# Between attention and the first expert layer: four weight loads issued later, two gathers moved into one branch, three buffers cleared at another place

## The chip, the cores and the metric

The kernel runs on one core of a Trainium2 chip. The metric is the time of one execution on the device in microseconds (us), the median of several runs. Five engines work side by side, each with its own queue of instructions that it takes in order: TensorE (PE, matrix products and transposes), VectorE (DVE), ScalarE (ACT), GpSimd (POOL) and SyncE (SP). SP and POOL also start transfers between main memory and on-chip memory: SP the plain ones, POOL the indirect ones, which read or write rows at addresses that stand in a table. Instructions wait for each other by counters.

## The reference

Attention over 2 x 8 heads of 576 positions with a mask in blocks of 64, then two layers of mixture of experts with 8 experts each, on 1152 tokens of 512 values (inner width 1024; `capacity` is 288):

```python
    scores = scale * np.matmul(q, k.transpose(0, 1, 3, 2))
    mask = block_i >= block_j
    scores = np.where(mask, scores, -1000000000.0)
    scores = scores - np.max(scores, axis=-1, keepdims=True)
    attn = np.exp(scores)
    attn = attn / (np.sum(attn, axis=-1, keepdims=True) + 1e-09)
    return np.matmul(attn, v).astype(np.float32)
...
    logits = x @ w_gate
    expert_idx = np.argmax(logits, axis=1)
...
        if counts[e] < capacity:
            disp[e, counts[e]] = x[i]
...
    h = np.maximum(np.einsum('ecd,edf->ecf', disp, w1), 0.0)
    y = np.einsum('ecf,efd->ecd', h, w2)
...
            out[i] = gate_w[i] * y[expert_idx[i], pos[i]]
```

Here `gate_w` is the softmax value of the chosen expert. The second layer works on the result in the same way, but sends each token to the two experts with the highest noisy logits and adds their weighted outputs.

## The kernel before

The kernel works in three stages one behind the other: attention, the eight experts of the first layer, the eight of the second. The stretch of this study is the seam between the first two.

**Weights.** Each expert has eight units of 512 KB, four of `w1` and four of `w2`. A unit is loaded by SP into one of seven buffers `raw0` to `raw6` (`load`, lines 148 to 159), and then split into a high part (ACT, line 167) and a low part (DVE, in two halves, line 170), which PE reads. As soon as DVE is through with a buffer, `split` issues the load that comes next into the same buffer (`behind(u)`). The last unit of each expert is not split; it goes to a buffer `wf` of its own. Units are numbered through the experts; `turn[u]` is the place of a unit in the order of splits. `HELD` (6) and `AHEAD` (5) are the first eleven places: those units are split during attention. Five of their buffers are loaded again behind the last rows of attention, with the units at the places 13 to 17; those at 14 to 17 are the four `w1` units of expert 2, which are split beside the work of expert 1.

**Attention's end.** The rows of attention are stored to main memory (`x_d`, lines 405 and 406). A table `T1` says which rows belong to which expert. The first 128 rows of expert 0 are also picked out directly on PE (L822), so that expert 0 can begin before anything has been fetched. The other rows are fetched by POOL with `row1(e, blk, n)` (line 1441), in blocks of 128, 128 and 32 rows, into `xr[e, blk]`, which has two sets of buffers (even and odd experts). Rows beyond an expert's count are left out by a bounds check.

**The experts of layer 1.** For each expert there are two branches, one for up to 128 tokens (`one_block`; its lines 1043 to 1080) and one for more (`large`, with `blocks`). Before the branch stands what both share. Inside a branch a planner (`Flow`) puts the operations of expert e, the splits of the weights for the next expert (`splits`), the transposes of the next expert's fetched rows (`prep`, lines 1015 to 1021), and the after-work of the expert before (`post`) into one order for each engine, by estimated costs. Its estimate of when a load has landed is a table (`came`), which the change does not touch. The result of expert e is scaled into `px` on ACT (line 1206), which reads the gate from the fetched rows `xr[e, 0]`.

**Three buffers `gs`** take the rows that layer 2 fetches. They are cleared once by POOL (line 1546).

Of the kernel before, what the change touches and what calls it, by code (L numbers as in the profile page):

```python
# [46 lines left out]
def attention_moe_moe2(ctx, tc, q, k, v, wg1, w1a, w2a, cap, wg2, wn2, noise, w1b, w2b, out):  # L47
    nc = tc.nc
    B, H, S, D = q.shape
    E, DM, F = w1a.shape  # L50
# [4 lines left out]
    XW = DM + 12  # L55
# [4 lines left out]
    SLOTS, RAWS, MORE = 13, 5, 2  # L60
# [5 lines left out]
    EARLY, HELD = 8 - WHOLE, 6  # L66
# [69 lines left out]
    def behind(u):  # L136

        i = turn[u] + (RAWS if turn[u] < HELD else RAWS + MORE)
        return order[i] if i < len(order) else None
# [8 lines left out]
    def load(u, q=nc.sync):  # L148
        if u is None or u >= NU:
            return  # L150
        m, r = divmod(u, 8 * E)
        e, i = divmod(r, 8)
        w1, w2 = (w1a, w2a) if m == 0 else (w1b, w2b)
        t = wfull[u % 8 - EARLY] if whole(u) else raw(u)
        if i < 4:
            q.dma_start(out=t, in_=w1[e, i * 128:(i + 1) * 128, :])
        else:
            f = (i - 4) * 256
            q.dma_start(out=t.rearrange("p (a d) -> p a d", a=2),
                              in_=w2[e, f:f + 256, :].rearrange("(a p) d -> p a d", p=128))  # L160

    def split(u, part=None, follow=True):
        if u >= NU:
            return
        t, h, l = raw(u), whi[slot(u)], wlo[slot(u)]
        if part in (None, 0):
            nc.scalar.activation(h, t, AF.Copy)  # L167
        if part != 0:
            c = {1: slice(0, 512), 2: slice(512, 1024), 3: slice(0, 1024), None: slice(0, 1024)}[part]
            (nc.gpsimd if part == 3 else nc.vector).tensor_sub(l[:, c], t[:, c], h[:, c].bitcast(F32))  # L170

            if part != 1 and follow:
                load(behind(u))

    def w1_at(e, kk, f0, f1):
        s = slot(8 * e + kk)
# [120 lines left out]
    with ExitStack() as actx:  # L297
# [564 lines left out]
        def split_op(i, deps=(), after=()):  # L862
            u = order[i]
            a = AT.add("split", "A", 0.95, lambda op: split(u, 0), list(deps) + [made["raw", i]])
            v1 = AT.add("split", "V", 0.6, lambda op: split(u, 1), [a], behind=after)
            made["split", i] = AT.add("split", "V", 0.6, lambda op: split(u, 2, False), [v1, a])
            made["raw", i + RAWS] = AT.add("load", "S", 0.1, lambda op: load(behind(u)), [made["split", i]], dma=1.5, drawn=False, behind=[made["stored"]] if i >= HELD else ())

        ctx.enter_context(tc.manual_schedule())
        made["load", 0] = AT.add("load", "S", 0.0, lambda op: None, dma=6.0, lag=-3.6)  # L870
# [568 lines left out]
    def row1(e, blk, n):  # L1439
        t = xr[e, blk] = xrs[e % 2][blk]  # L1440
        others("read", "sent", nc.gpsimd.indirect_dma_start(
            out=t[:n], out_offset=None, in_=x_d, in_offset=_off(T1[:n, 3 * e + blk:3 * e + blk + 1]),
            bounds_check=NT - 1, oob_is_err=False))

    for u in range(EARLY, 8):
        load(u)
    for e, i in ((1, 0), (0, 1), (0, 2), (1, 1), (1, 2), (0, 0)):
        row1(e, *BLK[i])
    nc.vector.memset(T2[:, 0], float(NT))
    nc.vector.memset(T2[:, 1], 0.0)  # L1450
    for _, _, t in pend[0:2]:
# [18 lines left out]
    for e in range(E):  # L1470
        for u in range(8 * e + EARLY, 8 * e + 8) if e else ():
            load(u)
        if e + 1 == E:
            F = Flow()
            total(F, cnt0, None)
            F.run()

        def beside(F, first):
            done = splits(F, units(e))
            nxt = post(F, first, last=True)[0] if first is not None else None  # L1480
            if e + 1 < E:
                for blk, n in BLK:
                    d = F.add("G", 1.04, lambda blk=blk, n=n: row1(e + 1, blk, n)) if e else None
                    prep(F, lambda blk=blk: xr[e + 1, blk], n, xT[(e + 1) % 2], 128 * blk, deps=[d], when=(WHEN0 if e == 0 else F.par["when"]) + 1.5 * blk)
            else:
                d, _ = rows2(F, (0, 0), 0, 0, tis[0])
                prep(F, lambda: G[0, 0][2], 128, xT[0], 0, deps=[d])
            return done, nxt

        last = None if e == 0 else pend[(e - 1) % 2]  # L1490
        cur = pend[e % 2]
        mt = [xr[e, i][:, DM:XW] for i in range(3)]
        n_e = many1(e)
        if e == 0:
            for r in regs[0].handles:
                nc.reg_load(r, cnt1[0:1, 0:1])

        def busy(bank, n):

            for _ in range(n):  # L1500
                nc.tensor.matmul(bank, hT[0][:, 0, 0:128], whi[slot(8 * e + 4)][:, 0:512], start=True, stop=True)

        def begin(F):

            def go():
                for r in regs[(e + 1) % 2].handles:
                    nc.reg_load(r, cnt1[0:1, e + 1:e + 2])
                tc.mark_branch_hint_location(f"first{e + 1}", hint=many1(e + 1) > 128, engines=[mybir.EngineType.PE])

            if e + 1 < E:  # L1510
                F.add("P", 0.4, go, tail=30.0, after=2.5)

        def large():
            F = Flow(LARGE)
            begin(F)
            done, nxt = beside(F, last)

            def fin(y, blk, p, first):
                r = to_pend(F, y, 128, lambda: mt[blk], 3 * e + blk, (pend[2], cur)[blk], p, first)
                if blk == 0:  # L1520
                    post(F, pend[2], deps=r, ranks=nxt)

            here = [prep(F, lambda blk=blk: xr[0, blk], n, xT[0], 128 * blk) for blk, n in BLK[1:]] if e == 0 else ()
            blocks(F, e, xT[e % 2], R, fin, done=done, deps=here)
            F.close(F.run())
            with tc.If(n_e > 256):
                F = Flow()
                _, z, _, tl = post(F, cur)
                product2(F, e, 2, lambda y, blk, p, first: to_pend(F, y, R, lambda: mt[2], 3 * e + 2, cur, p, first, deps=[z, tl["sent"]]))
                w = F.add("P", 1.6, lambda b: busy(b, 7), ends, take="h")  # L1530
                F.add("P", 0.0, lambda: None, [w], frees=w)
                F.run()

        with tc.If(n_e > 128, label=f"first{e}") as cmp:
            large()
        with cmp.Else():
            F = Flow(SMALL if e else FIRST)
            begin(F)
            done, nxt = beside(F, last)
            one_block(F, e, xT[e % 2], 128, lambda y, n, p, first: to_pend(F, y, n, lambda: mt[0], 3 * e, cur, p, first), done=done)  # L1540
            F.close(F.run())
        came, later = later, ({}, {})
        state["u"] = min(NU, 8 * e + 8 + EARLY)
        if e == 0:
            for i in range(3):
                nc.gpsimd.memset(gs[i], 0.0)


    mctx.close()
# [262 lines left out]
```

## Time and profile before

| | us |
|---|---|
| median of 3 runs (lowest, highest) | 547.79 (546.66, 547.98) |
| the profiled execution's own time | 548.82 |
| its span, first to last instruction | 547.2 |
| PE busy | 514.5 (94%) |
| DVE busy | 379.1 (69%) |
| ACT busy | 294.1 (54%) |
| POOL busy | 143.1 (26%) |

The profile comes from one execution. Its times count from the start of the span, which is 1.6 us shorter than the time of that execution. In the profile attention lasts to about 140 us, layer 1 to about 330, layer 2 to the end. In a row of a timeline the releaser in brackets is what ended the idle time before the instruction.

### The profile page before, as it was taken

Reading aid. Unit: us, or ns where it says so; the run is one execution under the profiler, and the core shown is the slowest. Engines: PE = TensorE matmul, PEld = TensorE weight load, DVE = VectorE, ACT = ScalarE, POOL = GpSimd, SP = SyncE. Lnnn points to the kernel's source line nnn. Section 1 sums busy time; section 2 is a strip of 40 time slices with the busy share of each in tenths; the row PEclk is TensorE's granted clock in tenths of the full one; section 3 lists DMA queues with packets and bytes.
Section 4 is the critical chain, followed back from the end, with each engine's and each line's share of the span. In section 5 each row is a group of like instructions: output and inputs, shape, how many; then the busy total and the mean of one; then the engine's idle time right before and its main releaser. Section 6 shows DMA issues by size and latency. Waiting matters only on the chain. (4 is left out here: it accounts for less than half of the span.)

```text
span 547.2 us, 10101 instructions
## 1 busy us (share of the span) xinstructions
PE 514.5 (94%) x3381; PEld 421.4 (77%) x3381; DVE 379.1 (69%) x1008; ACT 294.1 (54%) x580; POOL 143.1 (26%) x225
## 2 busy tenths in 40 slices
PE   3999999999978999999999998999999999999996
PEld 2777777877755876796975976888889797789794
DVE  6889988898748887867575567647657492658441
ACT  5888878882355776653544346335536171726130
POOL 3000000000355344313423224114415051455031
PEclk9999999999999999999999999999999999999999
DMA  6988987501667788754642444528585674285120
GB/s 136 217 196 244 243 224 177 173 2 65 225 213 267 241 264 280 269 181 133 208 123 77 133 151 141 182 90 282 208 299 192 225 264 175 79 311 190 66 67 35
DMA packets 71176, 99.17 MB, mean 181 GB/s; under 512 B 37130, under 2 KB 40586, under 8 KB 71088
## 3 DMA queue, kind: packets, MB, share of 16 engines
q1 hardware_dynamic: 63600, 83.16, 48.4%
q0 software_dynamic: 6432, 14.71, 8.7%
q8 instruction: 39, 0.64, 0.5%
q14 instruction: 49, 0.40, 0.3%
q10 hardware_dynamic: 1056, 0.26, 0.2%
HBM read 87.53 MB, written 12.25 MB: 182 GB/s over the span
## 5 line engine op out<-in xcount | busy, mean ns | idle before, releaser
L170 DVE TENSOR_TENSOR wl<-raw,wh 128x512 fp32r<-128x512 f32 x140 | 91.5, 684 | 12.9 <-ACT wh L167 12.6
L167 ACT ACTIVATE wh<-raw 128x1024 fp32r<-128x1024 f32 x70 | 71.2, 1052 | 20.6 <-PEq L1776 12.5
L170 DVE TENSOR_TENSOR both<-raw,both 128x512 fp32r<-128x512 f32 x100 | 66.0, 684 | 9.0 <-ACT both L167 8.5
L167 ACT ACTIVATE both<-raw 128x1024 fp32r<-128x1024 f32 x50 | 51.4, 1054 | 10.0 <-PEq L1776 8.3
L198 PE MATMUL h<-xh,wh 128*128 128x256 f32 (+1 forms) x184 | 52.8, 287 | 0.5
L199 PE MATMUL h<-xl,wh 128*128 128x256 f32 (+1 forms) x184 | 52.6, 286 | 0.0
L200 PE MATMUL h<-xh,wl 128*128 128x256 f32 (+1 forms) x184 | 52.5, 285 | 0.0
L1018 ACT ACTIVATE xh<-tp 128x512 fp32r<-128x512 f32 (+1 forms) x37 | 18.9, 536 | 56.3 <-PE tp L1015 54.6
L1583 POOL DMA_INDIRECT out_dram<-o,T2i x16 | 18.6, 1164 | 99.7 <-DVE o L1580 97.6
L1021 DVE TENSOR_TENSOR xl<-tp,xh 128x512 fp32r<-128x512 f32 (+1 forms) x37 | 21.8, 609 | 31.1 <-ACT xh L1018 30.9
L1145 ACT ACTIVATE hh<-h 128x512 fp32r<-128x512 f32 (+1 forms) x46 | 24.1, 523 | 34.7 <-PE h L200 29.8
L198 PE MATMUL h<-xh,both 128*128 128x256 f32 (+1 forms) x136 | 39.1, 288 | 2.7 <-DVE hl L1148 1.4
L1148 DVE SCALAR_TENSOR_TENSOR hl<-h,hh 128x512 fp32r<-128x512 f32 (+1 forms) x46 | 27.4, 596 | 18.0 <-ACT hh L1145 16.9
L199 PE MATMUL h<-xl,both 128*128 128x256 f32 (+1 forms) x136 | 39.0, 287 | 0.0
L200 PE MATMUL h<-xh,both 128*128 128x256 f32 (+1 forms) x136 | 38.8, 285 | 0.0
L198 PE MATMUL y<-wh,hh 128*128 128x512 f32 (+1 forms) x94 | 38.3, 408 | 0.0
L200 PE MATMUL y<-wh,hl 128*128 128x512 f32 (+1 forms) x94 | 37.0, 394 | 0.0
L199 PE MATMUL y<-wl,hh 128*128 128x512 f32 (+1 forms) x94 | 37.0, 394 | 0.0
L526 PE MATMUL s<-both 128*128 128x256 f32 (+2 forms) x128 | 33.0, 370 | 4.2 <-ACT both L468 2.5
L550 ACT ACTIVATE pt<-s,negmax 128x128 f32<-128x128 f32 (+3 forms) x64 | 33.4, 526 | 6.3 <-DVE negmax L537 5.1
L198 PEld LDWEIGHTS h<-xh,wh 128*128 128x128 f32 x184 | 34.7, 189 | 1.9 <-issue 1.6
L1437 POOL MEMSET xr<- 128x524 f32 x3 | 1.5, 547 | 132.2 <-DVE T1f L811 132.2
(295 smaller groups left out, 1331.1 us busy)
## 6 DMA issues: line engine op xcount, KB each, us to landing
raw<-in_moe_w_dram SPq DMA_DIRECT2D x120, 512.0 KB, 5.5
wf<-in_moe_w_dram SPq DMA_DIRECT2D x8, 512.0 KB, 4.3
out_dram<-zero SPq DMA_DIRECT2D x3, 768.0 KB, 5.7
both<-both SPq DMA_DIRECT2D x14, 160.0 KB, 2.7
raw<-in_q_dram SPq DMA_DIRECT2D x16, 128.0 KB, 4.3
vn<-in_v_dram SPq DMA_DIRECT2D x16, 128.0 KB, 2.6
both<-both SPq DMA_DIRECT2D x14, 144.0 KB, 2.6
raw<-in_k_dram SPq DMA_DIRECT2D x14, 128.0 KB, 4.6
```

What stands on the lines that cost most here:

```text
L167: nc.scalar.activation(h, t, AF.Copy)
L170: (nc.gpsimd if part == 3 else nc.vector).tensor_sub(l[:, c], t[:, c], h[:, c].bitcast(F32))
L198: nc.tensor.matmul(o, sh, mh, start=first, stop=False)
L199: nc.tensor.matmul(o, sh, ml, start=False, stop=False)
L200: nc.tensor.matmul(o, sl, mh, start=False, stop=last)
L526: nc.tensor.matmul(o, w[:, i, h, 128 * t:128 * t + 128], w[:, i + 2, h, 64 * h:64 * h + n], start=(i == 0), stop=(i == 1))
L550: nc.scalar.activation(o, i, AF.Exp, bias=negmax[:, pr, 2 * t + h:2 * t + h + 1], accum_out=ssum[b][:, t, 2 * p + h:2 * p + h + 1])
L1018: nc.scalar.activation(xh[:, :, c0:c0 + n], h["tp"][:, :, :n], AF.Copy)
L1021: nc.vector.tensor_tensor(xl[:, :, c0:c0 + n], h["tp"][:, :, :n], xh[:, :, c0:c0 + n].bitcast(F32), op=OP.subtract)
L1145: nc.scalar.activation(part(hfull[0], g - (KF - 2 * WHOLE) // per) if plain(g) else part(hh, g), of(g), AF.Relu)
L1148: nc.vector.scalar_tensor_tensor(part(hl, g), of(g), 0.0, part(hh, g).bitcast(F32), op0=OP.max, op1=OP.subtract)
L1583: ins = nc.gpsimd.indirect_dma_start(out=out, out_offset=_off(G[key][1][:n, 0:1]), in_=G[key, "o"][:n], in_offset=None, bounds_check=NT - ...
```

## The change

Four things are changed.

- Four loads that were issued behind attention's last store (`load(behind(u))` for the places 7 to 10 of the order) are issued inside expert 0's branch, behind the load that follows the split at place 11.
- The gathers of expert 0's second and third block move into the branch for more than 128 tokens.
- That leaves four gathers in front of the branch: the three of expert 1 and the first of expert 0, in that order.
- The three buffers `gs` are cleared right behind these gathers, no longer behind expert 0.

```diff
--- before.py
+++ after.py
@@ -171,6 +171,9 @@
 
             if part != 1 and follow:
                 load(behind(u))
+                if turn[u] == HELD + AHEAD:
+                    for i in range(1, AHEAD):
+                        load(behind(order[HELD + i]))
 
     def w1_at(e, kk, f0, f1):
         s = slot(8 * e + kk)
@@ -864,7 +867,8 @@
             a = AT.add("split", "A", 0.95, lambda op: split(u, 0), list(deps) + [made["raw", i]])
             v1 = AT.add("split", "V", 0.6, lambda op: split(u, 1), [a], behind=after)
             made["split", i] = AT.add("split", "V", 0.6, lambda op: split(u, 2, False), [v1, a])
-            made["raw", i + RAWS] = AT.add("load", "S", 0.1, lambda op: load(behind(u)), [made["split", i]], dma=1.5, drawn=False, behind=[made["stored"]] if i >= HELD else ())
+            if i <= HELD:
+                made["raw", i + RAWS] = AT.add("load", "S", 0.1, lambda op: load(behind(u)), [made["split", i]], dma=1.5, drawn=False, behind=[made["stored"]] if i >= HELD else ())
 
         ctx.enter_context(tc.manual_schedule())
         made["load", 0] = AT.add("load", "S", 0.0, lambda op: None, dma=6.0, lag=-3.6)
@@ -1444,8 +1448,10 @@
 
     for u in range(EARLY, 8):
         load(u)
-    for e, i in ((1, 0), (0, 1), (0, 2), (1, 1), (1, 2), (0, 0)):
+    for e, i in ((1, 0), (1, 1), (1, 2), (0, 0)):
         row1(e, *BLK[i])
+    for i in range(3):
+        nc.gpsimd.memset(gs[i], 0.0)
     nc.vector.memset(T2[:, 0], float(NT))
     nc.vector.memset(T2[:, 1], 0.0)
     for _, _, t in pend[0:2]:
@@ -1489,7 +1495,7 @@
 
         last = None if e == 0 else pend[(e - 1) % 2]
         cur = pend[e % 2]
-        mt = [xr[e, i][:, DM:XW] for i in range(3)]
+        mt = [xrs[e % 2][i][:, DM:XW] for i in range(3)]
         n_e = many1(e)
         if e == 0:
             for r in regs[0].handles:
@@ -1511,6 +1517,9 @@
                 F.add("P", 0.4, go, tail=30.0, after=2.5)
 
         def large():
+            if e == 0:
+                for blk, n in BLK[1:]:
+                    row1(0, blk, n)
             F = Flow(LARGE)
             begin(F)
             done, nxt = beside(F, last)
@@ -1541,9 +1550,6 @@
             F.close(F.run())
         came, later = later, ({}, {})
         state["u"] = min(NU, 8 * e + 8 + EARLY)
-        if e == 0:
-            for i in range(3):
-                nc.gpsimd.memset(gs[i], 0.0)
 
 
     mctx.close()
```

What the change makes of the queues is shown at three places, in the order of the built program. The names are tiles with a number of the build; in brackets is what the row waits for. `DMAHW0` to `DMAHW7` are eight counters that SP's transfers use in turn; before a transfer on SP goes out, the one before it on the same counter must have landed, so of the counters in a row of SP below the `DMAHW` is the row's own. `DMASW` are POOL's counters. When the two branches of an expert use a counter for different transfers, an instruction behind the branch waits for the counters of both.

SP in the program before, from the last store of attention to the branch of expert 0:

```order
L406 DMA x_d_63<-xrow1_124 64x140 [waits DMAHW1_49]
L159 DMA raw1_68<-in_moe_w2_dram 128x2x512 [waits DMAHW2_49]
L156 DMA raw2_69<-in_moe_w1_dram 128x1024 [waits DMAHW3_49]
L156 DMA raw3_70<-in_moe_w1_dram 128x1024 [waits DMAHW4_49]
L156 DMA raw4_71<-in_moe_w1_dram 128x1024 [waits DMAHW5_49]
L156 DMA raw0_67<-in_moe_w1_dram 128x1024 [waits DMAHW6_49]
L159 DMA wf0_1746<-in_moe_w2_dram 128x2x512 [waits DVE_49,DMAHW7_49,PE_49,Activation_49]
```

SP in the changed program, the small branch of expert 0 and the `wf` behind it; between the last store and the branch there are now only the loads of `raw1_68` and `wf0`:

```order
L159 DMA raw5_72<-in_moe_w2_dram 128x2x512 [waits DMAHW4_49,DVE_49,Activation_49]
L156 DMA raw2_69<-in_moe_w1_dram 128x1024 [waits DMAHW5_49]
L156 DMA raw3_70<-in_moe_w1_dram 128x1024 [waits DMAHW6_49]
L156 DMA raw4_71<-in_moe_w1_dram 128x1024 [waits DMAHW7_49]
L156 DMA raw0_67<-in_moe_w1_dram 128x1024 [waits DMAHW0_49]
L159 DMA raw6_73<-in_moe_w2_dram 128x2x512 [waits DMAHW1_49,DVE_49,Activation_49]
L159 DMA raw1_68<-in_moe_w2_dram 128x2x512 [waits DMAHW2_49,DVE_49,Activation_49]
L1543 UNCONDITIONAL_BRANCH
L159 DMA wf0_1742<-in_moe_w2_dram 128x2x512 [waits DMAHW3_49,PE_49]
```

The loads of `raw2`, `raw3`, `raw4` and `raw0` have moved from in front of the branch to the places two to five of seven in it; counter 7 is now that of `raw4`, counter 0 that of `raw0`, and counter 1 that of `raw6`.

POOL before, from the clearing of expert 0's buffers to the branch of expert 0 (`xr10` is expert 1, first block, `xr01` expert 0, second block):

```order
L1437 MEMSET xr00_1748 128x524 [waits PE_49,DVE_49,Activation_49,Pool_49]
L1437 MEMSET xr01_1749 128x524
L1437 MEMSET xr02_1750 128x524
L1441 DMA xr10_1751<-x_d_63,T1_88 128x524 [waits DMAHW1_49,DMAHW6_49,DMAHW0_49,DMAHW7_49,DVE_49,Pool_49]
L1441 DMA xr01_1749<-x_d_63,T1_88 128x524 [waits Pool_49]
L1441 DMA xr02_1750<-x_d_63,T1_88 32x524 [waits Pool_49]
L1441 DMA xr11_1752<-x_d_63,T1_88 128x524 [waits DVE_49]
L1441 DMA xr12_1753<-x_d_63,T1_88 32x524 [waits DVE_49]
L1441 DMA xr00_1748<-x_d_63,T1_88 128x524
L1496 TENSOR_LOAD cnt1_91 [waits DVE_49]
L1534 COMPARE_AND_BRANCH
```

POOL in the changed program, the same place:

```order
L1441 MEMSET xr01_1745 128x524
L1441 MEMSET xr02_1746 128x524
L1445 DMA xr10_1747<-x_d_63,T1_88 128x524 [waits DMAHW1_49,DMAHW6_49,DMAHW0_49,DMAHW7_49,DVE_49,Pool_49]
L1445 DMA xr11_1748<-x_d_63,T1_88 128x524 [waits DVE_49]
L1445 DMA xr12_1749<-x_d_63,T1_88 32x524 [waits DVE_49]
L1445 DMA xr00_1744<-x_d_63,T1_88 128x524 [waits Pool_49]
L1454 MEMSET g0_1736 128x524 [waits DMAHW4_49,DMAHW3_49,DMAHW5_49,DMAHW2_49,PE_49]
L1454 MEMSET g1_1737 128x524
L1454 MEMSET g2_1738 128x524
L1502 TENSOR_LOAD cnt1_91 [waits DVE_49]
L1543 COMPARE_AND_BRANCH
```

The gathers of `xr01` and `xr02` are gone from here, those of `xr11`, `xr12` and `xr00` stand two places earlier, and the clearing of `g0` to `g2` follows them.

ACT before, the start of expert 1's small branch: three splits, and then the relu `yT`:

```order
L167 ACTIVATE wh5_99<-raw4_71 128x1024 [waits DMAHW5_49,PE_49]
L167 ACTIVATE both0_106<-raw0_67 128x1024 [waits DMAHW6_49,PE_49]
L167 ACTIVATE wh4_98<-raw3_70 128x1024 [waits DMAHW4_49,PE_49]
L1507 TENSOR_LOAD cnt1_91
L1043 ACTIVATE yT_1724<-h0_1714 128x512 [waits PE_49,Activation_49]
```

ACT in the changed program, the same place:

```order
L167 ACTIVATE wh5_99<-raw4_71 128x1024 [waits DMAHW0_49,DMAHW7_49,PE_49]
L167 ACTIVATE both0_106<-raw0_67 128x1024 [waits DMAHW1_49,PE_49]
L167 ACTIVATE wh4_98<-raw3_70 128x1024 [waits DMAHW6_49,PE_49]
L1513 TENSOR_LOAD cnt1_91
L1047 ACTIVATE yT_1720<-h0_1710 128x512 [waits PE_49,Activation_49]
```

The order is the same. The first split (`raw4`) waits for the counters 0 and 7, where it waited for 5; the second (`raw0`) waits for counter 1, where it waited for 6.

## Rows read from the trace of the kernel before

**Rows 1.** Page, busy us by engine; then span and mean granted clock

```profile
PE 514.5 (94%) x3381; PEld 421.4 (77%) x3381; DVE 379.1 (69%) x1008; ACT 294.1 (54%) x580; POOL 143.1 (26%) x225
...
core 0: 547.2 us, clock 0.999
```

**Rows 2.** Who waited for whom, PE, whole span: us, times, longest us

```profile
PE tp L1015 <- DMA xr<-x_d,T: 3.6, 3, 1.7
...
PE s L526 <- ACT both L468: 2.5, 1, 2.5
```

**Rows 3.** Timeline of PE: start us, us, line, count [idle before <-releaser]

```profile
151.55 0.48 PE L1080 MATMUL y<-wh,hl 128*128 128x512 f32 x1
152.99 0.66 PE L1015 MATMUL tp<-ident,xr 128*128 128x128 f32 x4 [0.96 <-DMA xr<-x_d,T]
...
155.55 0.63 PE L1015 MATMUL tp<-ident,xr 128*128 128x128 f32 x4 [0.98 <-DMA xr<-x_d,T]
...
157.69 0.40 PE L1015 MATMUL tp<-ident,xr 32*128 32x32 f32 x4 [0.18 <-DVE xl L1021]
...
162.65 0.40 PE L200 MATMUL h<-both,xl 128*128 128x512 f32 x1
163.71 0.66 PE L1048 MATMUL tp<-ident,yT 128*128 128x128 f32 x4 [0.67 <-ACT yT L1043]
...
172.36 0.66 PE L1015 MATMUL tp<-ident,xr 128*128 128x128 f32 x4 [1.68 <-DMA xr<-x_d,T]
```

**Rows 4.** Timeline of POOL

```profile
146.33 1.22 POOL L1441 DMA_INDIRECT xr<-x_d,T  x1 [2.72 <-DVE xr L1437]
...
151.78 1.41 POOL L1441 DMA_INDIRECT xr<-x_d,T  x1 [0.30 <-DVE wl L170]
153.49 1.02 POOL L1441 DMA_INDIRECT xr<-x_d,T  x1 [0.30 <-issue]
...
160.34 1.49 POOL L1546 MEMSET g<- 128x524 f32 x3 [0.16 <-issue]
...
165.48 1.35 POOL L1441 DMA_INDIRECT xr<-x_d,T  x1 [0.28 <-issue]
```

**Rows 5.** All gathers into xr: time from issue to landing

```profile
DMA to landing us min/median/max: 2.5/5.0/6.8
```

**Rows 6.** Timeline of SP's transfers, each row's first issue

```profile
141.20 0.60 SPq L159 DMA_DIRECT2D raw<-in_moe_w_dram  x1
141.84 2.49 SPq L156 DMA_DIRECT2D raw<-in_moe_w_dram  x4
144.50 0.38 SPq L159 DMA_DIRECT2D wf<-in_moe_w_dram  x1
150.66 2.16 SPq L159 DMA_DIRECT2D raw<-in_moe_w_dram  x3
...
348.30 0.37 SPq L159 DMA_DIRECT2D raw<-in_moe_w_dram  x1
348.91 2.12 SPq L156 DMA_DIRECT2D raw<-in_moe_w_dram  x4
```

**Rows 7.** Timeline of ACT

```profile
159.65 0.69 ACT L1206 ACTIVATE px<-y,xr 128x512 f32<-128x512 f32 x1 [1.25 <-DMA xr<-x_d,T]
160.23 1.05 ACT L167 ACTIVATE wh<-raw 128x1024 fp32r<-128x1024 f32 x1
...
163.08 0.58 ACT L1043 ACTIVATE yT<-h 128x512 f32<-128x512 f32 x1
```

**Rows 8.** Landing of issues at 348.95, 350.75 and 144.5; then L156, 135 to 190

```profile
raw<-in_moe_w_dram SPq DMA_DIRECT2D x1, 512.0 KB, 6.0
...
raw<-in_moe_w_dram SPq DMA_DIRECT2D x1, 512.0 KB, 8.1
...
wf<-in_moe_w_dram SPq DMA_DIRECT2D x1, 512.0 KB, 9.4
...
DMA to landing us min/median/max: 3.7/6.0/8.3
```

## The prediction

> **What bounds the kernel now.** I read the page's busy row first: TensorE (PE) is busy 94% of the span, at a granted clock of 0.999 [rows 1]. So the change can only pay where PE stands still. The list of what PE waited for, over the whole span, gives the sum that the change can touch [rows 2]: the transposes of fetched rows (L1015) waited 3.6 us for the gathers `xr<-x_d`, in three pieces. That is about the most that the change can win.
>
> The timeline of PE places them [rows 3]. Expert 0 runs its small branch (L1048 belongs to `one_block`). PE is through with its work at 152.03 and starts the first L1015 at 152.99, 0.96 later; the second stands 0.98 for the same reason. The third is put down to VectorE (DVE), 0.18, but its gather, issued at 151.78, could well have landed only then; I count it with the gathers. That makes 2.12 us at the end of expert 0. In expert 1 a transpose (L1048) stands 0.67 us for ScalarE (ACT), and the last L1015, at 172.36, 1.68 us for the rows of expert 2: PE had nothing to do from 170.68 on. These pieces make up the 3.6, so behind 172.36 PE waits for no gather of this kind any more.
>
> **What the change removes.** POOL's timeline [rows 4]: six gathers are issued from 146.33 to 153.49, so 1.43 us apart; the first cannot go earlier, since it stands behind DVE's clearing, which waits for the stored rows, and nothing of that is changed. The two that go (expert 0's second and third block) stood second and third, so the other rows of expert 1 are asked for at about 147.8 and 149.2 instead of as the fourth and the fifth (151.78), and expert 0's own rows at about 150.6 in place of 153.49. Gathers here land in 2.5 to 6.8 us, half of them within 5.0 [rows 5]; with four loads less in front, PE finds its three blocks there. Bounds: 2.12 us won if all have landed, 0 if they take as long as now. I take 2.12: even 5.0 us after 146.33 is before 152.03, and the second block is wanted at 155.55 - 0.98 - 0.96 = 153.6, 5.8 after its issue. PE then has finished the first half of expert 1's layer at 163.05 - 2.12 = 160.93.
>
> **What it adds: loads that are now late.** In the timeline of SP four loads are issued from 141.84 on [rows 6]. The splits of expert 1, from 160.23 on, read them some 18 us later [rows 7]. Now they stand in SP's queue of the small branch, behind the load after the first split, which goes out at 150.66; with the two loads that also stood there, seven go out in about four microseconds. Their issue on SP costs nobody anything, as SP has nothing else queued but `wf`, whose turn comes when PE is through with the last one. But ACT wants them: its first three rows in expert 1 are splits, at 160.23 and 0.95 apart, and the relu `yT`, for which PE waits, stands behind them in the same queue and started at 163.08 [rows 7]. With PE and the rows of expert 0 earlier, ACT is free by 158.2 (its copy `px` at 159.65 took 0.69 us and moves by the 2.12, or by more, as it had waited for expert 0's rows). Then the landing decides. By the waits that the build lists (the ACT rows of the change above), the first split wants the fifth of the seven loads too, and the second split wants the sixth: both counters are shared with the other branch.
>
> When do the fifth and the sixth land? The nearest row is the five-load burst at 348.30: its fifth load, issued at about 350.7, landed after 8.1, so 10.5 us after the burst began [rows 6, 8]. The second had landed at 354.9 by the same view (6.0 after 348.91), so the three behind it took 1.3 us each; a sixth would be at 11.8. The other burst is the one that the change takes apart: a load at 141.20, the four, and `wf` at 144.50. `wf`, its sixth, landed 9.4 us after its own issue, so 12.7 after the first [rows 6, 8]; it had the stored rows ahead of it, which the new burst has not. I take 10.5 and 11.7, since gathers are under way in all three. The fifth is then there at 161.2, the sixth at 162.4.
>
> ACT: first split 161.2 to 162.15, second 162.4 to 163.35, third to 164.3, `yT` at 164.3 in place of 163.08: **1.2 us later** than before, although PE came 2.12 us earlier. So the 2.12 us go into a longer wait of PE for ACT (0.67 + 2.12 + 1.2 = 4.0 us), and 1.2 us more are lost. Bounds: the quickest load of this stretch took 3.7 [rows 8]; 3.7 and five steps of 1.3 make 10.2 for the sixth, and `yT` is then at 162.8, 0.3 earlier than before. From above 12.7, and 0.7 more for a gather in between (about half a load of bytes): `yT` at 166.0, 2.9 later.
>
> **What it wins back in expert 1.** Clearing the three buffers took POOL 1.49 us at 160.34, in front of the gather of expert 2's rows [rows 4], and POOL came to it only when expert 0's rows had landed, which ACT's wait puts at about 159.6 [rows 7]. Both get out of the way: the clearing now follows the four gathers, at about 152 to 153.5, where POOL would wait for those rows anyway; if this cover were gone it would cost its 1.49 us there. The gather of expert 2 waits next for ACT's last reading of expert 0's rows, by 158.2, and has some arithmetic of POOL in front; I put it at 160.5, 5 us before its present 165.48. PE is at that point at 170.68 + 1.2 = 171.9; such a gather has landed at 167.3 even with the 6.8 us of the slowest [rows 5]. So the 1.68 us vanish. Bounds: all of it, or nothing if the seven loads hold the gather up; I take all.
>
> Nothing else moves. In attention two splits change places on DVE and two loads of the same 512 KB on SP, with PE's and ACT's rows as before: 0. The removed gathers fetched only rows beyond the count, and are not run in this branch. The order of PE, ACT and DVE behind the attention is untouched, and with PE at 94% and no gather waited for behind 172.36 an offset in expert 1 stays an offset to the end.
>
> **The sum.** +1.2 at `yT`, which swallows the 2.12, and -1.68 at the gather: **-0.5 us**. Against the profiled execution's own 548.82 us (span 547.2 and 1.6 around it) that is 548.3; that execution was 1.0 above the median of the three runs, 547.79, so I forecast **547.3**.
>
> **A rule on landing.** The rows above give 1.3 us for each queued load and 3.7 or more for a first. The Trainium skill's page "DMA: Bandwidth & Descriptors", section "Anatomy of one DMA", fits a transfer as 2.0 us and its bytes at 436 GB/s; it was fitted on another issuing path. An estimate by that page is 9.2 us for six queued loads, so `yT` would be at 161.8, and the sum -3.0. The traces bear it out badly (10.5 for five), so the sum goes by the rows.
>
> **Rivals.**
> *The loads are there in time, or the splits don't wait for them* (faster). If the fifth and sixth land 1.3 us sooner, or the first split waits for the fourth load alone, `yT` is at 163.1 or earlier, and the sum is -1.7 or better; with no wait at all for loads it is -2.12 - 1.68 = -3.8, 544.0. For it: the gathers that slowed both bursts are fewer. Against it: both measured bursts. 0.30.
> *The long wait lets the clock fall* (slower). PE would stand 4.0 us before `yT`. The longest idle of PE inside this trace, 2.5 us (L526 behind ACT) [rows 2], went with a clock that stayed at 2.4 GHz, as the mean of 0.999 shows [rows 1]; 4.0 has no row. If the grant fell to 1.2 GHz, what follows takes up to twice as long: PE works from 163.71 to 170.68 almost without a stop, so up to 7 us are at stake, and half of it is 3.5: 547.3 + 3.5 = 550.8. It decides for slower once more than 2.1 us are lost. The Trainium skill's page "TensorE: Matmul & The Clock Gate", section "HAM oscillation", warns of idle gaps of PE that a wait for DMA makes, after which the next stretch starts cold; no run here shows it yet. 0.10, and 0.05 more for a sixth load that lands over 2 us later than I put it.
> *The gather of expert 2 is held up by the seven loads* (the change doesn't give back the 1.68): sum +1.2, 549.0, no change that shows. Against it: 11 us between issue (160.5) and need (171.9). 0.10.
> My own case has 0.45.
>
> **From these to the numbers.** A difference of 0.3% (1.6 us) is about what a measurement of this kernel can tell from none, so faster means under 546.15 and slower over 549.4. Faster: the first rival and a little of my case's lower end (-2.0), 0.33. Slower: 0.15. Same: 0.52. My own case spans 545.8 to 549.0 by its bounds (-2.0 to +1.2); the range for 8 in 10 takes in half of the first rival: 545.0 to 549.3.
>
> **What would show it.** Right: no idle before the first two L1015 of expert 0's end; the first split of expert 1 waiting for `raw`, at about 161; PE idle some 4 us before L1048, by ACT; no wait of L1015 for expert 2's rows. Wrong: splits of expert 1 at 158 to 160 with no wait (first rival); the granted clock under 1 behind the wait (second); L1015 still waiting near 172 (third).

## The result, and the profile after

| | before | after |
|---|---|---|
| median of 7 runs each (lowest, highest), us | 547.55 (546.02, 548.43) | 551.79 (549.62, 554.12) |
| ratio to before, with its 95% interval | | 1.0094 (1.0070 to 1.0118) |
| the profiled execution's own time, us | 548.82 | 554.12 |

The change makes the kernel slower, by 4.2 us between the medians. The profiled execution after is the slowest of its seven, which has to be kept in mind when its rows are read. Lines move by three or four: L1019 and L1052 are the L1015 and L1048 of before, L1047 is `yT`, L201 to L203 are L198 to L200. From the page of after, PE's busy row and then its span and clock, beside [rows 1]:

```profile
PE 519.2 (94%) x3381; PEld 426.5 (77%) x3381; DVE 379.3 (69%) x1008; ACT 294.6 (53%) x580; POOL 137.8 (25%) x223
...
core 0: 552.4 us, clock 0.990
```

PE runs the same 3381 instructions and is busy 4.7 us longer: its matmuls have become slower somewhere, and the mean granted clock has gone from 0.999 to 0.990. Of the 4.7 us, 1.6 lie at the end of attention and were not made by the change (last section); most of the rest lies in expert 1. What PE waited for over the whole span (us, times, longest) tells the other half; the line of the gathers [rows 2] is gone, and this one is new:

```profile
PE tp L1052 <- ACT yT L1047: 5.4, 1, 5.4
```

The timeline of PE after (start us, us, line, count, idle before and its releaser) answers to [rows 3]:

```profile
153.33 0.60 PE L1019 MATMUL tp<-ident,xr 128*128 128x128 f32 x4
...
154.76 0.60 PE L1019 MATMUL tp<-ident,xr 128*128 128x128 f32 x4
...
161.60 0.40 PE L203 MATMUL h<-both,xl 128*128 128x512 f32 x1
167.38 1.11 PE L1052 MATMUL tp<-ident,yT 128*128 128x128 f32 x4 [5.39 <-ACT yT L1047]
...
170.43 0.63 PE L202 MATMUL h<-both,xh 128*128 128x512 f32 x1
...
176.80 0.60 PE L1019 MATMUL tp<-ident,xr 128*128 128x128 f32 x4
```

No transpose of fetched rows waits any more, neither at expert 0's end nor for expert 2's rows. But PE stands 5.39 us in one piece before `yT`'s transposes, and behind it a matmul of 128x512 takes 0.63 us in place of 0.40. The windows of after show why (the stretch, its length in us, busy time and count of PE, PEld, DVE, ACT and POOL, then the granted clock as a share of 2.4 GHz, the busy share of the DMA engines, and GB/s):

```profile
160.00:164.00 4.00, 2.00 (x11) 1.34 (x9) 0.00 (x0) 0.43 (x1) 2.07 (x3) 1.00 1.01 375
164.00:168.00 4.00, 0.62 (x3) 0.62 (x4) 3.03 (x5) 3.78 (x6) 0.00 (x0) 0.80 0.54 168
168.00:172.00 4.00, 4.00 (x16) 3.61 (x15) 3.21 (x10) 2.95 (x6) 0.00 (x0) 0.50 0.84 313
172.00:176.00 4.00, 4.00 (x16) 3.20 (x16) 2.27 (x7) 2.24 (x3) 0.00 (x0) 0.84 0.49 157
```

The granted clock falls to its lower level, 1.2 GHz, during the idle time, and it is back at 2.4 GHz almost 7 us later (the matmuls take 0.40 us again from 173.35 on). Where the idle time comes from is seen on ACT and SP. ACT after, which answers to [rows 7]:

```profile
158.13 0.69 ACT L1210 ACTIVATE px<-y,xr 128x512 f32<-128x512 f32 x1 [0.78 <-PE y L187]
163.57 1.06 ACT L167 ACTIVATE wh<-raw 128x1024 fp32r<-128x1024 f32 x1 [4.75 <-DMA raw<-in_moe_w_dram]
164.84 1.06 ACT L167 ACTIVATE both<-raw 128x1024 fp32r<-128x1024 f32 x1 [0.22 <-DMA raw<-in_moe_w_dram]
165.81 1.04 ACT L167 ACTIVATE wh<-raw 128x1024 fp32r<-128x1024 f32 x1
166.75 0.58 ACT L1047 ACTIVATE yT<-h 128x512 f32<-128x512 f32 x1
```

SP's transfers after, beside [rows 6]:

```profile
152.12 0.38 SPq L159 DMA_DIRECT2D raw<-in_moe_w_dram  x1
152.54 1.89 SPq L156 DMA_DIRECT2D raw<-in_moe_w_dram  x4
154.55 0.90 SPq L159 DMA_DIRECT2D raw<-in_moe_w_dram  x2
```

Seven loads go out from 152.12 on, and ACT has nothing to do from 158.8 to 163.57, when the load that its first split wants is there. `yT` stands behind three splits. POOL after, beside [rows 4], has the clearing in time that nobody misses, and asks for expert 2's rows at 155.29 instead of 165.48:

```profile
149.36 1.02 POOL L1445 DMA_INDIRECT xr<-x_d,T  x1 [0.31 <-issue]
150.38 1.51 POOL L1454 MEMSET g<- 128x524 f32 x3
...
155.29 1.14 POOL L1445 DMA_INDIRECT xr<-x_d,T  x1 [0.28 <-issue]
```

### The profile page after: what moved, and what is told of

Same layout as the page of the kernel before. It is cut to its first block, busy times and chain, and to the rows that moved or that the text cites. A ratio compares the mean times of both kernels' runs of the same rounds, so it can differ in the third digit from the quotient of the medians.

```text
span 552.4 us, 10093 instructions
## 1 busy us (share of the span) xinstructions
PE 519.2 (94%) x3381; PEld 426.5 (77%) x3381; DVE 379.3 (69%) x1008; ACT 294.6 (53%) x580; POOL 137.8 (25%) x223
## 5 line engine op out<-in xcount | busy, mean ns | idle before, releaser
L201 PE MATMUL h<-xh,wh 128*128 128x256 f32 (+1 forms) x184 | 52.9, 288 | 0.6
L203 PE MATMUL h<-xh,wl 128*128 128x256 f32 (+1 forms) x184 | 52.5, 285 | 0.0
L201 PE MATMUL h<-xh,both 128*128 128x256 f32 (+1 forms) x136 | 39.3, 289 | 2.8 <-DVE hl L1152 1.5
L203 PE MATMUL h<-xh,both 128*128 128x256 f32 (+1 forms) x136 | 38.8, 285 | 0.0
L201 PE MATMUL y<-wh,hh 128*128 128x512 f32 (+1 forms) x94 | 38.3, 407 | 0.0
L203 PE MATMUL y<-wh,hl 128*128 128x512 f32 (+1 forms) x94 | 37.0, 394 | 0.0
L201 PEld LDWEIGHTS h<-xh,wh 128*128 128x128 f32 x184 | 34.7, 189 | 2.2 <-issue 1.6
```

Of the source, the lines that this page charges most:

```text
L201: nc.tensor.matmul(o, sh, mh, start=first, stop=False)
L203: nc.tensor.matmul(o, sl, mh, start=False, stop=last)
```

## The experiments

The theory: the late loads hold up ACT's queue, PE stands still for that, and the idle time lets the clock fall, so that PE's next stretch is slow as well; fewer gathers are a gain. The rivals: that the gathers' or the clearing's new place costs the time, that the clock fell for another reason than the idle time, or that only the wait costs. Ratios are to the kernel before on the same chip: the first four runs share one chip (before: median 546.25 of 32 runs), the last four another (547.24 of 23).

**All loads early again.** The late loads are taken out of the change:

```diff
-                if turn[u] == HELD + AHEAD:
-                    for i in range(1, AHEAD):
-                        load(behind(order[HELD + i]))
...
-            if i <= HELD:
-                made["raw", i + RAWS] = AT.add("load", "S", 0.1, lambda op: load(behind(u)), [made["split", i]], dma=1.5, drawn=False, behind=[made["stored"]] if i >= HELD else ())
+            made["raw", i + RAWS] = AT.add("load", "S", 0.1, lambda op: load(behind(u)), [made["split", i]], dma=1.5, drawn=False, behind=[made["stored"]] if i >= HELD else ())
```

> The change with its first part undone: the four loads of raw rows are issued in attention again, while the fewer gathers and the moved clearing stay. My theory (the late loads block ScalarE's queue, and TensorE's idle time then lets the clock fall; the rest of the change gains) expects: no wait of ScalarE for raw in expert 1, no wait of L1015's transposes for gathers at the end of expert 0 (2.12 us before) nor for expert 2's rows (1.68 us before), yT some 2 us earlier than before's 163.08, granted clock 1.00 from 164 to 174, and 2 to 3.8 us less than before: 544 to 546. Rival (moving the gathers or the clearing is what costs): slower than before also here, with new waits on GpSimd or for gathers, 549 or more. Rival (the gathers were not what TensorE waited for): as before, within 1 us.

Measured: 544.60 median, ratio 0.9969 (0.9953 to 0.9986), 1.7 us under before. Its timeline of PE:

```profile
161.93 0.66 PE L1048 MATMUL tp<-ident,yT 128*128 128x128 f32 x4 [0.19 <-ACT yT L1043]
...
168.70 0.60 PE L1015 MATMUL tp<-ident,xr 128*128 128x128 f32 x4
```

In this profile there is no wait for gathers, none of ACT for `raw`, and the clock is at 1.00 from 140 to 180 us. So the moved gathers and clearing gain, and the loss is in the late loads. The gain is a little under what was expected; the second profile of before and the run with `yT` repeated show below what may be missing. From the first of these rows to the second PE works without a stop: 6.77 us at 2.4 GHz, the measure for all that follows. In the profile after the same stretch lasts from 167.38 to 176.80, 9.42 us.

**The late loads alone.** The same lines, added to the kernel before with nothing else:

```diff
+                if turn[u] == HELD + AHEAD:
+                    for i in range(1, AHEAD):
+                        load(behind(order[HELD + i]))
```

> The kernel before with the late loads alone; gathers and clearing as before. My theory expects: the splits of expert 1 wait for raw until about 163.5 and 164.8 less what attention's end is earlier, TensorE stands 3 us or more before L1048, the clock falls to half behind it for some microseconds, and the time is 1.5 to 5 us over before: 549 to 553. As the gathers of expert 0's end now follow none of the four loads, up to 1 us of the 2.12 us may be won back. Rival (the gathers' move is the cause): as before within 1 us. Rival (the clock's fall needs a longer idle than this one, as TensorE arrives 2 us later than in the change): clock at 1.00, time 0 to 2 us over before.

Measured: 551.85, ratio 1.0088 (1.0061 to 1.0114), as much as the whole change. First issue of its burst, by SP's timeline, then ACT's, then PE's:

```profile
151.84 0.38 SPq L159 DMA_DIRECT2D raw<-in_moe_w_dram  x1
```

```profile
162.27 1.06 ACT L167 ACTIVATE wh<-raw 128x1024 fp32r<-128x1024 f32 x1 [3.74 <-DMA raw<-in_moe_w_dram]
163.55 1.06 ACT L167 ACTIVATE both<-raw 128x1024 fp32r<-128x1024 f32 x1 [0.22 <-DMA raw<-in_moe_w_dram]
...
165.46 0.58 ACT L1047 ACTIVATE yT<-h 128x512 f32<-128x512 f32 x1
```

```profile
166.09 1.03 PE L1052 MATMUL tp<-ident,yT 128*128 128x128 f32 x4 [4.38 <-ACT yT L1047]
...
175.96 0.60 PE L1019 MATMUL tp<-ident,xr 128*128 128x128 f32 x4
```

PE's idle time is 4.38 us, and the measured stretch 9.87 us. One part of the expectation was too low: L1019 waits for no gather at the end of expert 0 here, although all six are issued as before. Taking the four loads out of their way was enough for the 2.12 us: the first gather lands 3.4 us after its issue, where it took 6.6 before. The change does both, and then loses it in the wait for the loads. The nine runs fall into two kinds: seven with a mean granted clock of 0.988 to 0.990 took 551.7 to 552.3, two with 0.998 and 0.999 took 547.42 and 548.69.

**The wait kept, PE kept busy in it.** In front of the transposes:

```diff
         def tr(j, bank):
+            if e == 1 and j == 0:
+                for _ in range(22):
+                    nc.tensor.matmul(bank, xh[:, 0, c], w1_at(e, 0, 0, 512)[0], start=True, stop=True)
```

> The change with 22 matmuls of 128x512 added in front of expert 1's first transposes of the first layer (L1048 before), which write a bank that the transposes then overwrite: work that is thrown away, about 5 us of it, in the time in which TensorE stands idle there. The wait for yT itself stays. Theory of the clock (the idle makes the grant fall, which costs 2.45 us on top of the wait): the granted clock stays at 1.00 from 164 to 174, the matmuls behind take 0.40 us again in place of 0.63, yT at the same place against the end of attention, and the time is 2 to 3 us below the change: 548.5 to 550. Rival (the clock falls for another reason, or only the wait costs): time as the change within 0.7 us, 551 to 552.5, or longer by what the added matmuls stand in the way.

Measured: 547.76, ratio 1.0038 (1.0019 to 1.0058); the change has 1.0094 in its own comparison, so 0.56% or 3.1 us are gone, slightly more than the 2 to 3 expected. None of the 12 runs has a mean clock under 0.995. PE's timeline, and two windows:

```profile
159.40 5.17 PE L1052 MATMUL tp<-both,xh 128*128 128x512 f32 x22
164.41 0.60 PE L1055 MATMUL tp<-ident,yT 128*128 128x128 f32 x4
...
178.23 0.47 PE L201 MATMUL h<-wh,xh 128*128 128x512 f32 x1 [0.95 <-ACT wh L167]
```

```profile
164.00:168.00 4.00, 4.00 (x25) 3.48 (x24) 3.82 (x10) 3.82 (x7) 0.00 (x0) 1.00 0.87 292
168.00:172.00 4.00, 4.00 (x22) 3.31 (x22) 3.65 (x13) 2.64 (x6) 0.00 (x0) 1.00 0.61 214
```

With the same late loads, on the same ACT queue, the clock stays up if PE works. What is left, 2.1 us over before, is the wait, the added matmuls (they end about 0.6 us after `yT` is usable), and a new wait further on: expert 2's first matmul stands 0.95 us for a split on ACT. Why that split is not there in time is not shown, and the profile after has no such wait.

**The late loads in the order in which they are wanted:**

```diff
-                    for i in range(1, AHEAD):
+                    for i in (3, 4, 2, 1):
```

> The change with the four late loads issued in the order in which expert 1's splits wait for them, so that the first split wants the third load of the burst instead of the fifth, and the second the fourth instead of the sixth; all loads still late. By 1.3 us for each queued load the first split comes 2.6 us earlier, at about 161, and yT at about 164.2 in place of 166.75 (the second half of the layer wants the remaining loads later and may wait a little). Theory of late loads and clock: TensorE's idle before L1048 shrinks from 5.4 to about 2.8 us, the time falls by 2.5 us if the clock still falls, and by about 5 us if it stays up: 549 or 547. Rival (the landing hangs on the whole burst, not on the place in it): as the change, 551 to 552.

Measured: 547.16, ratio 1.0012 (0.9987 to 1.0036). Five runs with a mean clock of 0.991 or 0.992 have a median of 549.08, seven with 0.995 and more one of 546.03: close to the two times expected, both in one kernel. The profiled execution is of the first kind. ACT's first two splits now wait for nothing and the third does, so that `yT` comes 20.87 us after PE's first matmul of expert 0 (162.37 - 141.50), in place of 23.05: as early as before (20.85), while PE is there 2.3 us sooner. So where the clock stays up nothing is won or lost, and where it falls 3 us are lost. ACT's row of the third split, then PE and one window:

```profile
161.41 1.06 ACT L167 ACTIVATE wh<-raw 128x1024 fp32r<-128x1024 f32 x1 [1.53 <-DMA raw<-in_moe_w_dram]
```

```profile
163.00 0.87 PE L1052 MATMUL tp<-ident,yT 128*128 128x128 f32 x4 [3.02 <-ACT yT L1047]
...
172.88 0.60 PE L1019 MATMUL tp<-ident,xr 128*128 128x128 f32 x4
```

```profile
164.00:168.00 4.00, 4.00 (x14) 3.42 (x15) 3.44 (x11) 3.15 (x6) 1.72 (x2) 0.50 0.80 252
```

The place of a load in the burst decides when its split can start. And with an idle time of about 3 us (measured in the one profiled execution) the clock falls in some executions and, by their mean clocks, not in others.

**A second profile of before.** Nothing is edited.

> The kernel before, unchanged, for a second profile of it. The gain of the change without its late loads came out at 0.31% in the times (1.7 us), but at 3.8 us in the spans of two profiled executions. Theory (the profile of before shows an execution above the median, with a late landing of the stored rows, so that its waits for gathers are longer than usual): here the first gather starts under 4.1 us behind the end of attention, and the waits of L1015 sum to 1.5 to 3 us in place of 3.6. Rival (the waits are always those of the first profile, and the missing 2 us are lost elsewhere): 3.3 us or more of waits. And if the grant of TensorE's clock dips at the end of attention (mean clock 0.995) in some executions of this kernel too, the dip in the profile of the change was not made by the change.

Measured: one execution, 545.63 us, clock 0.999. Its PE timeline:

```profile
152.48 0.66 PE L1015 MATMUL tp<-ident,xr 128*128 128x128 f32 x4 [1.25 <-DMA xr<-x_d,T]
...
155.20 0.63 PE L1015 MATMUL tp<-ident,xr 128*128 128x128 f32 x4 [1.14 <-DMA xr<-x_d,T]
...
157.34 0.40 PE L1015 MATMUL tp<-ident,xr 32*128 32x32 f32 x4 [0.20 <-DMA xr<-x_d,T]
...
169.68 0.60 PE L1015 MATMUL tp<-ident,xr 128*128 128x128 f32 x4
```

The waits at expert 0's end are here too (2.6 us, and the third is for a gather, as the prediction guessed), but there is no wait for expert 2's rows. The 1.68 us of [rows 3] belong to the execution that was profiled first, which was 1.0 us over its median; they are not in every run. This second execution is 1.6 us under the median of its chip, so neither of the two stands for the median run.

**The gathers alone.** All loads early, and the clearing back behind expert 0:

```diff
-    for i in range(3):
-        nc.gpsimd.memset(gs[i], 0.0)
...
         state["u"] = min(NU, 8 * e + 8 + EARLY)
+        if e == 0:
+            for i in range(3):
+                nc.gpsimd.memset(gs[i], 0.0)
```

> Of the change only the fewer gathers: the four loads in attention and the clearing of three buffers behind expert 0, as before. My theory (the clearing never stood on the path once the gathers are early) expects the time of the run with gathers and clearing moved, 1 to 2.5 us under before, the clearing on GpSimd right ahead of the gather of expert 2's rows, that gather 1.5 us later than with the clearing moved, and still no wait of TensorE for it. Rival (it was the clearing that held expert 2's rows up): the wait of 1.7 us stays, and the time is at most 1 us under before.

Measured: 544.68, ratio 0.9952 (0.9931 to 0.9973). POOL's timeline:

```profile
155.20 1.48 POOL L1549 MEMSET g<- 128x524 f32 x3 [0.21 <-remote]
...
158.21 1.13 POOL L1441 DMA_INDIRECT xr<-x_d,T  x1 [0.28 <-issue]
```

The gather of expert 2's rows is asked for at 158.21, over ten us before its transposes at 168.71, which wait for nothing. Where the clearing stands makes no difference that shows: the interval overlaps that of the run with both parts.

**A wait of PE without late loads.** All loads early, but `yT` is computed eleven times over:

```diff
         def relu(j):
-            nc.scalar.activation(hsb[j][:n], hp[j][:n], AF.Relu)
+            for _ in range(11 if e == 1 and j == 0 else 1):
+                nc.scalar.activation(hsb[j][:n], hp[j][:n], AF.Relu)
```

> All loads early again, gathers and clearing moved, and the relu yT for which TensorE waits in expert 1 is done eleven times over instead of once (the same result written again), so that TensorE stands idle some 5 us before the transposes with no late load anywhere. Theory (the idle itself makes the clock fall): granted clock at half for some 6 us behind the wait, and 4.8 us for the wait and 2.5 for the clock over the run without the repeats: 7 to 7.5 us, 1.0% over before. Rival (the clock fell because of the transfers under way, or of the load on the other engines): clock stays at 1.00, and 4.8 us over that run, 0.55% over before.

Measured: 553.72, ratio 1.0117 (1.0082 to 1.0151); 9.0 us over the run before this one. PE and two windows:

```profile
168.37 1.11 PE L1049 MATMUL tp<-ident,yT 128*128 128x128 f32 x4 [6.48 <-ACT yT L1044]
...
177.56 0.60 PE L1015 MATMUL tp<-ident,xr 128*128 128x128 f32 x4
```

```profile
164.00:168.00 4.00, 0.00 (x0) 0.00 (x0) 0.00 (x0) 3.81 (x7) 0.00 (x0) 0.87 0.78 250
168.00:172.00 4.00, 3.63 (x15) 3.44 (x16) 1.44 (x4) 3.20 (x6) 0.00 (x0) 0.50 0.03 13
```

The repeats took longer than I had put them, so the idle time is 6.48 us and not 5. The rest is as the theory has it: 6.3 us more of idle time, 9.19 - 6.77 = 2.4 us for the clock, 8.7 in sum. The clock falls late in the idle time, in the first of the two windows (a mean of 0.87), where the DMA share is 0.78; it then stays at half with next to no transfer under way (a share of 0.03). Transfers alone don't bring it down: in the run in which PE was kept busy it stayed at 1.00 at a share of 0.87. The two runs together show that here the idle time of PE made the clock fall, with the late loads or without.

This profile also has a wait for a gather, though no load is late and the gathers and the clearing are moved:

```profile
153.22 0.66 PE L1015 MATMUL tp<-ident,xr 128*128 128x128 f32 x4 [1.35 <-DMA xr<-x_d,T]
```

The first gather keeps its place in the queue in every kernel here. From its issue to its landing it takes 7.5 us in this profile, 7.4 and 8.1 in the other two with the gathers moved and all loads early, and 6.6 and 7.5 in the two of before; with all four loads late it takes 3.4 to 4.3 (the loads alone, reordered, PE kept busy). With all loads early PE escapes this wait only in the two profiles in which it is itself 1.6 us late at the end of attention (last section): there the gather has landed at 153.05 and 152.50, and PE begins at 153.07 and 153.06. So moving the gathers takes away the second wait and the third, and the late loads take away the first.

**Two late loads instead of four.** The two units that ACT's first two splits of expert 1 read are loaded in attention again:

```diff
-                    for i in range(1, AHEAD):
+                    for i in (2, 1):
                         load(behind(order[HELD + i]))
...
-            if i <= HELD:
+            if i <= HELD or i > HELD + 2:
```

> The change with two of its four late loads (those that the first two splits of expert 1 read) issued in attention as before, and the other two late, the one that the third split reads first. Theory (a late load costs only where its landing comes after its split's turn): first and second split wait for nothing, the third for the third load of the burst, which by some 8 us from the first issue is there at about its turn; no idle of TensorE over 1 us before L1048, clock at 1.00, and the time of the run with all loads early within 1 us: 1 to 2.5 us under before. Rival (any late load in this burst costs): 2 us or more over that run.

Measured: 544.92, ratio 0.9946 (0.9925 to 0.9967), 3.0 us under before by the ratio: faster than both kernels, and not to be told from the two runs with all loads early. ACT and PE:

```profile
157.01 1.05 ACT L167 ACTIVATE wh<-raw 128x1024 fp32r<-128x1024 f32 x1
157.96 1.05 ACT L167 ACTIVATE both<-raw 128x1024 fp32r<-128x1024 f32 x1
158.91 1.04 ACT L167 ACTIVATE wh<-raw 128x1024 fp32r<-128x1024 f32 x1
```

```profile
160.49 0.66 PE L1052 MATMUL tp<-ident,yT 128*128 128x128 f32 x4 [0.19 <-ACT yT L1047]
```

The three splits follow each other without a wait. Here the two loads that come late cost nothing, since they are there by their splits' turn.

## Why the prediction was wrong, step by step

It said 547.3 us and no change that shows; 551.79 was measured, outside of its range.

- **The gathers at expert 0's end (2.12 us)**: right. No L1019 waits there, after the change or in the other three profiles with all four loads late. What the prediction missed is that the late loads alone do this, so the two parts don't add, and that the moved gathers alone don't: the first wait stayed, 1.35 us with `yT` repeated.
- **The loads that are late, and `yT` 1.2 us later**: right in mechanism and nearly in size. The first split started 11.45 us behind the burst's first issue in the profile after (163.57 - 152.12), 10.43 in the run with the late loads alone (162.27 - 151.84); 10.5 was forecast. `yT` came 23.05 us behind PE's first matmul of expert 0 after the change (166.75 - 143.70), 22.07 with the loads alone (165.46 - 143.39), and 20.85 before (163.08 - 142.23): 2.2 and 1.2 us later. The larger figure is that of the slowest execution.
- **The clock**: this is the step that failed. The sum let the 4.0 us of idle time cost only themselves and left the clock at 2.4 GHz; that it falls was a rival with a chance of 0.10. It fell in six of the seven runs after the change, by their mean clocks, and cost 2.4 to 3.1 us (in the four profiles with the fall the stretch of 6.77 us took 9.19 to 9.88). The rival's own working, half of 7 us, was near: 550.8. The row used against it, 2.5 us of idle time at full clock [rows 2], was true, but it said nothing of 4.0. Nor was it the longest wait of PE in that view, which has this one:

```profile
PE tp L442 <- DMA raw<-in_k_dram: 5.7, 1, 5.7
```

It is the time before PE's first matmul of the span, so it doesn't show what a pause in the work does to the clock. The prediction named the Trainium skill's page "TensorE: Matmul & The Clock Gate", section "HAM oscillation", which warns of just this, a stretch that starts cold behind a wait of PE for DMA; the runs agree, here with ACT between the DMA and PE.
- **The 1.68 us won back at expert 2's rows**: the wait did vanish, but a second profile of before hasn't got it. So it can't be counted as a gain against the median run, and to subtract both this wait and the profiled execution's 1.0 us over the median may well count one thing twice; how many runs of before have the wait is not known.

Put together anew: 547.55, plus 1.2 for `yT`, plus 2.4 to 3.1 for the clock, is 551.2 to 551.9, where the measured median lies. Without the clock's fall the run with PE kept busy has 2.1 us over before, 0.6 of it from its own added matmuls; so even then the forecast of -0.5 would have been off by about 2 us. The 1.68 us and that run's wait of 0.95 us at expert 2's first matmul would be enough for it, but no run takes the two apart.

## What to carry to other kernels

When a move makes one idle time of TensorE longer than those that the trace shows between its matmuls, price the work behind it at half the clock (here a fall cost 2.4 to 3.1 us) and give that case a chance like the others'. In front of expert 1's transposes 0.2 us of idle time went with no fall in any profile, about 3 us with one in some runs, 5 us with one in nearly all. A load may be moved later as far as its reader's turn, so order late loads by who is wanted first, and look at what stands behind the reader in its queue. A wait in the profile of one execution is not yet a gain to be had: take a second profile, above all if the profiled run lies over the median.

## What was not expected of the hardware

**How surely the clock falls.** A fall in expert 1 alone shows as a mean clock of 0.991 or 0.992 (the profiles with `yT` repeated and with the loads reordered); with the second dip below it is 0.990 or less. By that the runs count as follows; the idle time of PE is that of each kernel's one profiled execution:

| kernel | idle us before `yT` | runs with the clock fallen |
|---|---|---|
| loads reordered | 3.02 | 5 of 12 |
| late loads alone | 4.38 | 7 of 9 |
| the change | 5.39 | 6 of 7 |
| `yT` repeated | 6.48 | 6 of 6 |

**A second dip, which the change did not make.** At the end of attention PE stands 1.21 us for `choice` in every profile. In the profile after, the clock fell there as well; PE's row, and a window within it:

```profile
135.13 6.55 PE L825 MATMUL s<-choice,xrow 128*128 128x128 f32 x40 [1.21 <-DVE choice L782]
```

```profile
136.00:140.00 4.00, 4.00 (x25) 4.00 (x24) 3.89 (x11) 0.00 (x0) 0.00 (x0) 0.61 0.19 54
```

In the second profile of before the same forty matmuls take 4.92 us with the clock at 1.00:

```profile
134.58 4.92 PE L822 MATMUL s<-choice,xrow 128*128 128x128 f32 x40 [1.21 <-DVE choice L779]
```

The profiles of the runs with all loads early and with the gathers alone have the dip and a mean clock of 0.995; that of the late loads alone has it beside the fall in expert 1 (0.989). 14 of the 32 runs of before on the first chip have a mean clock of 0.995 too, so by the mean clocks it comes and goes in a kernel that is not changed. The gathers alone change nothing that runs ahead of this place. It follows an idle time of only 1.2 us, so the idle time's length alone does not decide. What else does, no run here tells. Nor is it settled why those 14 runs of before were its faster ones (median 545.3, against 547.9 for the five with 1.000); that PE, being later, meets the gathers already landed would fit, but no profile of such a run was taken.

The same sorting changes how the gain of the moved gathers reads. On the second chip before has a median of 545.4 in its 7 runs with a mean clock of 0.995 or 0.996 and 547.3 in its 15 with 0.997 or more; the gathers alone have 545.2 (8 runs) and 543.5 (4). On the first chip before has 545.3 (17) and 547.1 (15), all loads early 545.6 (4) and 544.4 (8). So the gain, 3.9 and 2.8 us by these medians, lies in the executions without the dip; with it there is next to none.
